# Windowed attention beside a gated feed-forward: the value products of two chunks issued together

## The chip, the cores and the metric

The kernel runs on one NeuronCore of a Trainium2 chip. The metric is the device time of one execution in microseconds (us). Three executions of the kernel before took 825.59, 825.71 and 825.8 us; their median is 825.71 us. TensorE is called PE below, its weight loads PEld, VectorE DVE, ScalarE ACT, GpSimd POOL, and the engine that issues most of the transfers SP.

## The reference

Two branches read the same `x` (2048 rows, 512 columns) and are mixed row by row by a gate.

```python
qkv = (x @ wqkv).reshape(B, S, 3, H, Dh)            # H = 32 heads, Dh = 16
scores = einsum("bhqd,bhkd->bhqk", q, k) * Dh ** -0.5
mask = (i - j >= 0) & (i - j < 256)                 # each row sees itself and the 255 before
a = einsum("bhqk,bhkd->bhqd", softmax(scores), v) @ wo
b = (silu(x @ w_gate) * (x @ w_up)) @ w_down        # 1792 hidden columns
out = g * a + (1 - g) * b                           # g = sigmoid((x * gate_w).sum(-1))
```

Only the attention is touched by the change: the step that multiplies exponentials by values, and what turns its result into the attention's rows.

## The kernel before

Everything is float32; products of full precision are made of three products of split halves. The attention works on 8 groups of four heads (`G`), each over 16 blocks of 128 rows (`NB`). The rows are also counted in chunks of 512 (`NCH` = 4 for each group).

The middle of the kernel is one loop over `t` = 0 to 128 (line 601); `g, i = divmod(t, 16)` gives group and block, and each `t` has four head steps `hd` = 0 to 3. The order on every engine is the order in which the program writes the instructions (line 40). A head step writes, in this order:

- `stage1` of the next group (line 251): one matmul of raw scores (L263) into a `ps1` bank, and on DVE one instruction that adds the mask and takes the row maximum (L265);
- `stage2` of this group (line 293): one matmul of shifted scores, keys on the partitions (L304), into a `ps2` bank, and on ACT the exponential into a tile `pt` (L306). Each block needs two `pt` tiles, one for each pair of heads. After every second head POOL zeroes what lies outside the window (L308, L311);
- three pairs of matmuls of a side job (`lanes`, L215): either the projection of a later group or a piece of the feed-forward's hidden products, in accumulators `pa` and `pb`. A job lasts four `t`: its parts 0 and 2 fill the two `pa` tiles, its parts 1 and 3 the two `pb` tiles;
- whatever has been put in `AT` for this `(t, hd)` by `later`, and one step of `FIN`.

PSUM is shared out by lines 164 to 166: two tiles each under the names `pa`, `pb`, `ps1` and `ps2`, each 128x512 float32.

When a job's last part is over, `copies` (line 515) has ACT move its two tiles to SBUF (L519). For the two `pb` tiles this falls into the first `t` of the next job: the first tile at head step 0, the second at head step 2.

```python
for m in range(2):
    later(t0, 2 * m, lambda m=m: nc.scalar.copy(places[m], ps[m]))
```

At every fourth `t` (part 0, head step 1) `av` (line 316) writes one chunk's value products, "a run": 64 (chunk 0) or 96 small matmuls (L328) on a half of the rows and a quarter of the columns each. The lower half of the keys adds up in a tile `first`, named `pb` (`pa` for the very last run), the upper half in a tile `second`, named `ps2`. A chunk reads the exponentials of the six blocks that end with its own last one, and value tiles `vg` that `load_v` (line 288) fetches from DRAM.

`finish` (line 333) then has five steps: ACT copies `second` to SBUF (L339); DVE adds `first` (L341, and for chunk 0, where the upper half has no first 64 columns, a copy of these, L343); DVE transposes (L346); DVE divides by the sum that stands in column 16 of each head (L350, L351); DVE transposes back (L355) and POOL issues the transfer to `od`. It is a generator; line 616 takes a step of it at `(part, hd)` = (0, 2), (1, 1), (2, 1), (3, 1), after a first one right behind `av`.

The feed-forward's second product and the output projection follow after the loop (from line 638).

Of the kernel before, what the change touches and what calls it, by code (L numbers as in the profile page):

```python
# [9 lines left out]
F32 = mybir.dt.float32  # L10
F32R = mybir.dt.float32r
AF = mybir.ActivationFunctionType
ALU = mybir.AluOpType
# [3 lines left out]
P = 128  # L17
S, D, H, DH, W, F = 2048, 512, 32, 16, 256, 1792
NK = D // P
NB = S // P  # L20
CH = 512
NCH = S // CH
G = H // 4
NF = F // P
VW = 4 * (DH + 1) + DH
# [8 lines left out]
def gated_mix(ctx, tc, xT, xn, w01, wqk, wv, wo, wgu, wd, gw, out):  # L34
# [4 lines left out]
    nc = tc.nc  # L39
# [8 lines left out]
    od = dram.tile([G, P, S], F32, name="od")  # L48
# [40 lines left out]
    def run(gen, n=None):  # L89

        while n is None or n > 0:
            if next(gen, run) is run:
                break
            n = n and n - 1
# [74 lines left out]
    with ExitStack() as A:  # L169
        sm = A.enter_context(tc.tile_pool(name="sm", bufs=2))  # L170
# [59 lines left out]
        def proj(g, c, pool, name, todo=None, los=nc.gpsimd):  # L230

            hf, cc = divmod(c, 2)
            if cc == 0:
                X[g, hf] = x_pair() if g == hf else x_pair(vpool, f"x{g}{hf}")

            def done(ps):
                raw = kept()
                nc.scalar.copy(raw, ps)
                split_qk(g, hf, cc, raw, los)
            return whole(pool, name, todo or products(("p", g), c), done)  # L240

        def stack(g, hf):
            for pr in range(2):
                q, k = (halves_of(t[g % 2][pr])[hf] for t in (QT, KT))
                hi, lo = (x[32 * pr:] for x in X[g, hf])
                for b, (qx, kx) in enumerate(((hi, hi), (hi, lo), (lo, hi))):
                    nc.sync.dma_start(q[b::4].bitcast(F32), qx[:32].bitcast(F32))
                    nc.sync.dma_start(k[b::4].bitcast(F32), kx[64:96].bitcast(F32))

        MX = {}  # L250
        def stage1(g, qb):

            hf, b = divmod(qb, NB // 2)
            if b == 0:
                MX[g, hf] = sm.tile([P, 4, NB // 2], F32, name="mx")
            q0, k0 = qb * P, max(0, qb - 2) * P
            n = q0 + P - k0
            for hd in range(4):
                pr, j = divmod(hd, 2)
                r = slice(64 * j, 64 * j + 63)  # L260

                ps = ps2.tile([P, CH], F32, name="ps2") if g == 0 and pr else ps1.tile([P, CH], F32, name="ps1")
                nc.tensor.matmul(ps[:, :n], QT[g % 2][pr][r, q0:q0 + P], KT[g % 2][pr][r, k0:k0 + n],  # L263
                                 start=True, stop=True)
                mx = nc.vector.tensor_tensor_reduce(out=ps[:, :n], in0=ps[:, :n], in1=mask[:, 3 * P - n:],  # L265
                                                    scale=1.0, scalar=NEG, op0=ALU.add, op1=ALU.max,
                                                    accum_out=MX[g, hf][:, hd, b:b + 1])
                if g == 0:
                    BEHIND.append(mx)
                yield  # L270

        def put_max(g, hf):
            mt = sm.tile([P, 32], F32, name="mt")
            nc.vector.transpose(mt, MX[g, hf].rearrange("p h b -> p (h b)"))
            u = 2 * g + hf
            nc.sync.dma_start(mxd[u], mt)
# [7 lines left out]
                                      v[2 * pr + j:2 * pr + j + 1])  # L284

        VG, PT, AV = {}, {}, {}

        def load_v(n):

            VG[n] = sm.tile([P, 4, VW], F32, name="vg", bufs=4)  # L290
            nc.sync.dma_start(VG[n], vd[n // 4, :, n % 4 * 4:n % 4 * 4 + 4])

        def stage2(g, kb):
# [22 lines left out]
        def av(g, c):  # L316


            AV[g, c] = (pp.tile([P, CH], F32, name="pb" if 4 * g + c + 1 < len(UNITS) else "pa"),
                        ps2.tile([P, CH], F32, name="ps2"))  # L320

            orders = [[4 * c + m for m in ms if 4 * c + m >= 0] for ms in ((0, 1, 2, -1, -2, 3), (0, 1, -1, 2, 3, -2))]
            for n, kbs in enumerate(zip(*orders)):
                for j in range(4):
                    for h, (o, kb) in enumerate(zip(HALVES, kbs)):
                        k0 = kb * P + 64 * h
                        q0, q1 = max(k0, c * CH), min(k0 + W + 64, c * CH + CH)
                        nc.tensor.matmul(AV[g, c][h][32 * j:32 * j + 32, q0 - c * CH:q1 - c * CH],  # L328
                                         VG[4 * g + kb // 4][o, kb % 4, 17 * j:17 * j + 32],
                                         PT[g, kb, j // 2][o, j % 2, q0 - kb * P:q1 - kb * P],  # L330
                                         start=n == 0, stop=n == len(orders[0]) - 1, skip_group_check=True)

        def finish(g, c):


            first, second = AV[g, c]
            both = osb.tile([P, CH], F32, name="on")
            lo = 0 if c else 64
            nc.scalar.copy(both[:, lo:], second[:, lo:])  # L339
            yield  # L340
            nc.vector.tensor_tensor(out=both[:, lo:], in0=first[:, lo:], in1=both[:, lo:], op=ALU.add)  # L341
            if lo:
                nc.vector.tensor_copy(both[:, :lo], first[:, :lo])  # L343
            yield
            ot = osb.tile([P, CH], F32, name="on")
            nc.vector.transpose(ot, both)  # L346
            yield
            v = ot.rearrange("p (s e) -> p s e", e=32)
            rc = osb.tile([P, CH // 32], F32, name="rc", bufs=1)
            nc.vector.reciprocal(rc, v[:, :, DH])  # L350
            nc.vector.tensor_tensor(out=v[:, :, :DH], in0=v[:, :, :DH],  # L351
                                    in1=rc[:, :, None].to_broadcast([P, CH // 32, DH]), op=ALU.mult)
            yield
            on = osb.tile([P, CH], F32, name="on")
            nc.vector.transpose(on, ot)  # L355
            nc.gpsimd.dma_start(od[g, :, c * CH:(c + 1) * CH], on)
            yield

        vp = ExitStack()
        vpool = vp.enter_context(tc.tile_pool(name="vpool", bufs=1))  # L360
# [76 lines left out]
        both = [proj(g, 0, pp, "pa", [(w01raw[:, k, g], xraw[0][k]) for k in range(NK)]) for g in range(2)]  # L437
# [40 lines left out]
        first = chain(*(stage1(0, b) for b in range(NB)))  # L478
# [15 lines left out]
        for c in range(2, NCH):  # L494
            run(proj(1, c, pp, "pb"))
        stack(1, 1)
        for n in range(4):
            load_v(n)
        vp.close()
        ptp = A.enter_context(tc.tile_pool(name="ptp", bufs=13))  # L500
        osb = A.enter_context(tc.tile_pool(name="osb", bufs=2))


        AT = {}
# [1 line left out]
        def later(t, hd, *fs):  # L506
            AT.setdefault((t, hd), []).extend(fs)
# [89 lines left out]

        FIN, tops = iter(()), [(0, 1)]  # L600
        for t in range(G * NB + 1):
            g, i = divmod(t, NB)
            d, part = divmod(t, NSLOT)
            if part == 0:
                turns = unit(UNITS[d], t) if d < len(UNITS) else [iter(())] * NSLOT
            s1 = stage1(g + 1, i) if t < g7 else iter(())
            s2 = stage2(g, i) if t < G * NB else iter(())
            for hd in range(4):
                run(s1, 1)
                if t < g7:  # L610
                    run(s2, 1)
                elif hd % 2 == 0:
                    run(s2, 2)
                run(turns[part], 3)
                if (part, hd) in ((0, 2), (1, 1), (2, 1), (3, 1)):
                    run(FIN, 1)
                for f in AT.pop((t, hd), ()):
                    f()
                if hd == 1 and part == 0:
                    while tops:  # L620
                        top = tops.pop()
                        put_max(*top)
                        later(t + 1, 1, lambda top=top: get_max(*top))
                    if t:
                        ag, c = divmod(d - 1, NCH)
                        av(ag, c)
                        FIN = finish(ag, c)
                        run(FIN, 1)
            if i in (7, 15) and g + 1 < G:
                tops.append((g + 1, i // 8))  # L630
            if t >= 10 and t % 4 == 2 and t + 6 < G * NB:
                load_v((t + 6) // 4)
        run(FIN)
        for key in sorted(AT):
            for f in AT[key]:
                f()
# [1 line left out]
    with ExitStack() as B:  # L638
# [114 lines left out]
        second = []  # L753
        fresh, waiting, ready = [], [(0, n, *first_halves[n]) for n in range(2)], []
        for c, n in seq:
            f = ORDER[n]
            todo, ready, second = ready, second, []
# [58 lines left out]
```

## Time and profile before

| | |
|---|---|
| median of three executions | 825.71 us |
| the profiled execution | 825.82 us |
| its span, first to last instruction | 824.1 us |
| PE busy | 815.9 us (99%) |
| DVE busy | 509.8 us (62%) |
| ACT busy | 451.6 us (55%) |
| POOL busy | 343.1 us (42%) |
| value products (L328), matmuls | 2816 |
| runs of value products | 32, from 95.4 us to 599.6 us |

The span is what the profile sees; 1.7 us of the execution lie around it. Busy PE time is the time in which at least one matmul is under way by the profile; matmuls overlap, so the mean duration of one (346 ns for L328) is longer than the distance from one to the next. In the views of instructions in order of time, the columns are the start, the duration, engine, line, operation, tile written and read, shapes and count, and in brackets the idle time before it with what ended it.

### The profile page before, as it was taken

How to read it: one execution, taken by the hardware profiler on the slowest of the kernel's cores; microseconds unless marked ns; L12 is line 12 of the kernel's file. 1: busy time of each engine (PE TensorE's matmuls, PEld its weight loads, DVE VectorE, ACT ScalarE, POOL GpSimd, SP SyncE). 2: the span in 40 equal slices, each digit the busy share in tenths (PEclk: the TensorE clock that was granted, in tenths of full speed). 3: DMA queues.
4: the chain of work that ended last, by engine and by line, in shares of the span. 5: the costliest groups of instructions: out<-in, count | busy, mean ns of one | idle time of the engine just before them, and what ended most of it. 6: DMA issues, size and time to landing. Idle time of an engine off the chain costs nothing.

```text
span 824.1 us, 21565 instructions
## 1 busy us (share of the span) xinstructions
PE 815.9 (99%) x8306; PEld 677.6 (82%) x8306; DVE 509.8 (62%) x1422; ACT 451.6 (55%) x940; POOL 343.1 (42%) x631
## 2 busy tenths in 40 slices
PE   9999999999999999999999999999999999999998
PEld 6788988888888988887888888877778888888886
DVE  5496677677667676676677677745548443443443
ACT  6422666666666666666666666666647423334341
POOL 5812555555546555555554654456600111011020
PEclk9999999999999999999999999999999999999999
DMA  8484525625634643642652553556769444573621
GB/s 293 111 259 148 167 101 156 180 96 139 195 109 115 188 135 98 183 143 90 181 167 88 172 157 114 147 190 226 248 224 371 158 156 123 165 218 102 213 94 51
DMA packets 70582, 133.27 MB, mean 162 GB/s; under 512 B 14288, under 2 KB 19024, under 8 KB 70480
## 3 DMA queue, kind: packets, MB, share of 16 engines
q1 hardware_dynamic: 66512, 118.00, 46.4%
q0 software_dynamic: 3968, 13.90, 4.6%
q8 instruction: 65, 1.06, 0.5%
q14 instruction: 37, 0.30, 0.1%
HBM read 61.08 MB, written 45.61 MB: 129 GB/s over the span
## 4 chain that ended last, share of the span: by engine, by line
PE 88%; DMA 4%; POOL 3%; DVE 2%; SPq 1%; ACT 1%; issue 1%; ACTq 0%; POOLq 0%
PE pb L215 22%; PE pa L215 22%; PE pb L328 7%; PE ps L263 6%; PE ps L85 6%; PE ps L84 6%; PE ps L83 6%; PE ps L304 4%; PE pb L84 2%; PE pb L85 2%; PE pb L83 2%; PE ps L328 2%; DMA ev<-wd 1%; PE pb L708 1%; PE pa L708 1%
## 5 line engine op out<-in xcount | busy, mean ns | idle before, releaser
L265 DVE CUSTOM_DVE_ANT_0 ps<-ps,mask 128x384 f32<-128x384 f32 (+2 forms) x512 | 272.2, 540 | 142.5 <-PE ps L263 76.8
L306 ACT ACTIVATE pt<-ps 128x384 f32<-128x384 f32 (+2 forms) x512 | 240.8, 477 | 114.9 <-PE ps L263 56.8
L308 POOL TENSOR_SCALAR_AFFINE_SELECT pt<-pt 128x256 f32<-128x256 f32 x256 | 108.2, 423 | 212.5 <-ACT pt L306 204.0
L304 PE MATMUL ps<-q,k 64*128 64x384 f32 (+2 forms) x512 | 162.5, 328 | 0.0
L263 PE MATMUL ps<-k,q 63*128 63x384 f32 (+2 forms) x512 | 158.6, 330 | 0.0
L215 PE MATMUL pb<-xhi,wh 64*128 64x512 f32 x512 | 115.2, 394 | 0.0
L215 PE MATMUL pb<-xlo,wh 64*128 64x512 f32 x512 | 114.0, 391 | 0.0
L215 PE MATMUL pb<-xhi,wl 64*128 64x512 f32 x512 | 113.8, 392 | 0.0
L215 PE MATMUL pa<-xhi,wh 64*128 64x512 f32 x512 | 112.3, 393 | 0.0
L215 PE MATMUL pa<-xlo,wh 64*128 64x512 f32 x512 | 110.9, 391 | 0.0
L215 PE MATMUL pa<-xhi,wl 64*128 64x512 f32 x512 | 110.7, 391 | 0.0
L263 PEld LDWEIGHTS ps<-k,q 63*128 63x128 f32 x512 | 88.8, 185 | 16.1 <-issue 5.4
L311 POOL TENSOR_SCALAR_AFFINE_SELECT pt<-pt 128x256 f32<-128x256 f32 x224 | 98.7, 441 | 0.0
L304 PEld LDWEIGHTS ps<-q,k 64*128 64x128 f32 x512 | 93.0, 185 | 5.6 <-issue 0.8
L712 DVE TENSOR_TENSOR sg<-got,sg 128x512 f32<-128x512 f32 x50 | 44.5, 889 | 51.4 <-ACT sg L711 48.1
L328 PE MATMUL ps<-pt,vg 64*32 64x320 f32 (+4 forms) x1408 | 75.2, 346 | 0.0
L328 PE MATMUL pb<-pt,vg 64*32 64x320 f32 (+3 forms) x1360 | 74.0, 350 | 0.8 <-ACT ev L519 0.7
L265 DVE DVE_READ_ACCUMULATOR2_ANT mx<- 128x1 f32 x512 | 72.1, 141 | 0.0
L328 PEld LDWEIGHTS pb<-pt,vg 64*32 64x32 f32 x1360 | 46.5, 106 | 29.1 <-ACT pt L306 9.9
L215 PEld LDWEIGHTS pb<-xhi,wh 64*128 64x128 f32 x512 | 59.3, 185 | 8.6 <-ACT ev L519 0.3
L215 PEld LDWEIGHTS pb<-xhi,wl 64*128 64x128 f32 x512 | 59.3, 184 | 7.5
L215 PEld LDWEIGHTS pa<-xhi,wl 64*128 64x128 f32 x512 | 56.7, 184 | 7.9
(162 smaller groups left out, 1557.8 us busy)
## 6 DMA issues: line engine op xcount, KB each, us to landing
raws<-ev SPq DMA_DIRECT2D x104, 256.0 KB
got<-raws SPq DMA_DIRECT2D x100, 256.0 KB
od<-on POOLq DMA_DIRECT2D x32, 256.0 KB, 3.1
raw<-wgu SPq DMA_DIRECT2D x28, 256.0 KB
q<-xhi SPq DMA_DIRECT2D x56, 128.0 KB
k<-xhi SPq DMA_DIRECT2D x56, 128.0 KB
vd<-vs POOLq DMA_DIRECT2D x8, 672.0 KB, 5.9
vg<-vd SPq DMA_DIRECT2D x32, 168.0 KB
```

What stands on the lines that cost most here:

```text
L83: nc.tensor.matmul(ps, lh, rh, start=start and i == 0, stop=False)
L84: nc.tensor.matmul(ps, lh, rl, start=False, stop=False)
L85: nc.tensor.matmul(ps, ll, rh, start=False, stop=stop and i == n - 1)
L215: mm = nc.tensor.matmul(ps[me], w[r], x[r], start=not second and i == 0, stop=bool(second) and i == n - 1)
L263: nc.tensor.matmul(ps[:, :n], QT[g % 2][pr][r, q0:q0 + P], KT[g % 2][pr][r, k0:k0 + n], start=True, stop=True)
L265: mx = nc.vector.tensor_tensor_reduce(out=ps[:, :n], in0=ps[:, :n], in1=mask[:, 3 * P - n:], scale=1.0, scalar=NEG, op0=ALU.add, op1=ALU.m ...
L304: nc.tensor.matmul(ps[:, :n], KT[g % 2][pr][r, k0:k0 + P], QT[g % 2][pr][r, k0:k0 + n], start=True, stop=True)
L306: BEHIND.append(nc.scalar.activation(pt[:, j, :n], ps[:, :n], AF.Exp, scale=SCALE))
L308: nc.gpsimd.affine_select(out=pt[:, :, :P], in_=pt[:, :, :P], pattern=[[0, 2], [1, P]], compare_op=ALU.is_ge, fill=0.0, base=0, channel_mu ...
L311: nc.gpsimd.affine_select(out=pt[:, :, 2 * P:], in_=pt[:, :, 2 * P:], pattern=[[0, 2], [-1, P]], compare_op=ALU.is_ge, fill=0.0, base=-1, ...
L328: nc.tensor.matmul(AV[g, c][h][32 * j:32 * j + 32, q0 - c * CH:q1 - c * CH], VG[4 * g + kb // 4][o, kb % 4, 17 * j:17 * j + 32], PT[g, kb, ...
L712: nc.vector.tensor_tensor(out=sg, in0=gu[1], in1=sg, op=ALU.mult)
```

## The change

Chunks 0 and 1 of a group are multiplied at one place: when the eighth block of the group is through (`i` = 8). Chunk 2 stays at `i` = 12 and chunk 3 at `i` = 0 of the next group, so that a group has three runs in place of four. The places of the five steps of `finish` are written out as pairs (distance in `t`, head step); of chunk 0, the copy and the sum stand right behind the two runs, in the order copy of chunk 0, copy of chunk 1, sum of chunk 0. The exponentials of eight blocks and a half must now be kept: 17 tiles `pt` in place of 13. There are 3 buffers `vg` in place of 4, with loads at other times, 3 buffers `on` in place of 2, one fixed tile for the reciprocals, and the scratch for transfers that POOL issues is set to 4096.

```diff
-            VG[n] = sm.tile([P, 4, VW], F32, name="vg", bufs=4)
+            VG[n] = sm.tile([P, 4, VW], F32, name="vg", bufs=3)
...
+            place = {}
+            def copy():
+                both = place[0] = osb.tile([P, CH], F32, name="on")
+                nc.scalar.copy(both[:, lo:], second[:, lo:])
+            def add():
+                both = place[0]
+                nc.vector.tensor_tensor(out=both[:, lo:], in0=first[:, lo:], in1=both[:, lo:], op=ALU.add)
+                if lo:
+                    nc.vector.tensor_copy(both[:, :lo], first[:, :lo])
+            def across():
+                place[1] = osb.tile([P, CH], F32, name="on")
+                nc.vector.transpose(place[1], place[0])
...
+            return copy, add, across, divide, back
...
-        for n in range(4):
+        for n in range(3):
             load_v(n)
         vp.close()
-        ptp = A.enter_context(tc.tile_pool(name="ptp", bufs=13))
-        osb = A.enter_context(tc.tile_pool(name="osb", bufs=2))
+        ptp = A.enter_context(tc.tile_pool(name="ptp", bufs=17))
+        osb = A.enter_context(tc.tile_pool(name="osb", bufs=3))
...
-        FIN, tops = iter(()), [(0, 1)]
+        FIN, tops = {}, [(0, 1)]
+        LOADS = {9: 3, 13: 4, 17: 5, 18: 6}
+
+        def values(t):
+
+            ag, m = divmod(t - 8, NB)
+            if m == 0:
+                cs, times = (0, 1), [((0, 1),) * 2 + ((0, 3), (2, 0), (2, 3)), ((0, 1), (0, 2), (1, 1), (3, 2), (4, 1))]
+            else:
+                cs, times = (1 + m // 4,), [((0, 1), (0, 2), (1, 1), (2, 1), (3, 1))]
+            for c in cs:
+                av(ag, c)
+            for k, steps in enumerate(zip(*(finish(ag, c) for c in cs))):
+                for todo, ts in zip(steps, times):
+                    dt, hd = ts[k]
+                    if (dt, hd) == (0, 1):
+                        todo()
+                    else:
+                        FIN.setdefault((t + dt, hd), []).append(todo)
...
-                if (part, hd) in ((0, 2), (1, 1), (2, 1), (3, 1)):
-                    run(FIN, 1)
+                for f in FIN.pop((t, hd), ()):
+                    f()
                 for f in AT.pop((t, hd), ()):
                     f()
...
-                    if t:
-                        ag, c = divmod(d - 1, NCH)
-                        av(ag, c)
-                        FIN = finish(ag, c)
-                        run(FIN, 1)
+                    if t > 4 and i != 4:
+                        values(t)
...
-            if t >= 10 and t % 4 == 2 and t + 6 < G * NB:
-                load_v((t + 6) // 4)
-        run(FIN)
+            m = (t - 3) % NB + 3
+            if t > 8 and m in LOADS and (t - m) // 4 + LOADS[m] < 4 * G:
+                load_v((t - m) // 4 + LOADS[m])
...
-    nc = bacc.Bacc("TRN2", target_bir_lowering=False, num_devices=1)
+    nc = bacc.Bacc("TRN2", target_bir_lowering=False, num_devices=1, dynamic_dma_scratch_size=4096)
```

`av`, `copies` and the names and numbers of the PSUM tiles are the same before and after.

More of the change, by code (lines that the diff above doesn't have):

```diff
@@ L286, in gated_mix @@
         VG, PT, AV = {}, {}, {}
+        RC = sm.tile([P, CH // 32], F32, name="rc", bufs=1)
         def load_v(n):
-            VG[n] = sm.tile([P, 4, VW], F32, name="vg", bufs=4)
+            VG[n] = sm.tile([P, 4, VW], F32, name="vg", bufs=3)
             nc.sync.dma_start(VG[n], vd[n // 4, :, n % 4 * 4:n % 4 * 4 + 4])
@@ L336, in finish, with divide, back @@
             first, second = AV[g, c]
-            both = osb.tile([P, CH], F32, name="on")
             lo = 0 if c else 64
[L339 to L357, printed above, removed]
+            place = {}
[10 more added lines that the diff above has]
+                nc.vector.transpose(place[1], place[0])
+            def divide():
+                v = place[1].rearrange("p (s e) -> p s e", e=32)
+                nc.vector.reciprocal(RC, v[:, :, DH])
+                nc.vector.tensor_tensor(out=v[:, :, :DH], in0=v[:, :, :DH],
+                                        in1=RC[:, :, None].to_broadcast([P, CH // 32, DH]), op=ALU.mult)
+            def back():
+                on = osb.tile([P, CH], F32, name="on")
+                nc.vector.transpose(on, place[1])
+                nc.gpsimd.dma_start(od[g, :, c * CH:(c + 1) * CH], on)
+            return copy, add, across, divide, back
         vp = ExitStack()
@@ L623, in gated_mix @@
                         later(t + 1, 1, lambda top=top: get_max(*top))
-                    if t:
-                        ag, c = divmod(d - 1, NCH)
-                        av(ag, c)
-                        FIN = finish(ag, c)
-                        run(FIN, 1)
+                    if t > 4 and i != 4:
+                        values(t)
             if i in (7, 15) and g + 1 < G:
                 tops.append((g + 1, i // 8))
-            if t >= 10 and t % 4 == 2 and t + 6 < G * NB:
-                load_v((t + 6) // 4)
-        run(FIN)
+            m = (t - 3) % NB + 3
+            if t > 8 and m in LOADS and (t - m) // 4 + LOADS[m] < 4 * G:
+                load_v((t - m) // 4 + LOADS[m])
+        for key in sorted(FIN):
+            for f in FIN[key]:
+                f()
         for key in sorted(AT):
```

## The prediction

> **What bounds the kernel now.** I read the page's head and its chain first, then the busy time of a stretch out of the loop's middle, then what PE waited for.
>
> ```profile
> span 824.1 us, 21565 instructions
> PE 815.9 (99%) x8306; PEld 677.6 (82%) x8306; DVE 509.8 (62%) x1422; ACT 451.6 (55%) x940; POOL 343.1 (42%) x631
> PE 88%; DMA 4%; POOL 3%; DVE 2%; SPq 1%; ACT 1%; issue 1%; ACTq 0%; POOLq 0%
> ```
> ```profile
> 200.00:300.00 100.00, 100.00 (x1306) 85.81 (x1304) 70.18 (x234) 64.10 (x141) 54.52 (x111) 1.00 0.51 153
> ```
> ```profile
> PE pb L328 <- ACT ev L519: 0.7, 2, 0.4
> ```
>
> In the loop PE is busy 100 of 100 us at full clock (columns: stretch, length, then PE, PEld, DVE, ACT, POOL), DVE 70, ACT 64 and POOL 55. Over the whole kernel the value products let PE wait twice, 0.7 us in all. So in the loop every microsecond that PE gains or loses is one of the kernel's; work added to another engine costs nothing unless it makes PE wait.
>
> **What one run costs beside its products.** The instructions of PE in order of time, first an ordinary step, then the way into and out of a run of chunk 0:
>
> ```profile
> 174.87 0.39 PE L215 MATMUL pb<-xhi,wl 64*128 64x512 f32 x2
> 175.10 0.33 PE L304 MATMUL ps<-q,k 64*128 64x384 f32 x1
> ```
> ```profile
> 160.59 0.41 PE L215 MATMUL pa<-xhi,wl 64*128 64x512 f32 x2
> 160.93 0.45 PE L328 MATMUL pb<-pt,vg 64*32 64x320 f32 x1
> ...
> 162.47 0.42 PE L328 MATMUL pb<-pt,vg 64*32 64x128 f32 x8
> 162.81 0.44 PE L263 MATMUL ps<-k,q 63*128 63x384 f32 x1
> ```
>
> From the last pair of L215 to the next pair of scores it is 0.23 us (174.87 to 175.10); from there to the first value product 0.34 us (160.59 to 160.93). Entering a run costs 0.11 us more than an ordinary step. On leaving, L263 starts at 162.81, 0.08 us before the modelled end of the run's last product (162.47 + 0.42 = 162.89). If the second run followed the first with no wait, one entry and one leaving would be saved. No row shows two runs joined; I bound the leaving by nothing and by as much again as the entry: a gain of 0.11 to 0.22 us for each group, 0.9 to 1.8 us for eight. The products themselves stay: 2816 matmuls before and after.
>
> The Trainium skill has a rule for this saving: "TensorEngine Tiling (Array Packing)", Key Properties, says that changing the tiling mode drains TensorE. The trace agrees in kind, with the 0.11 us above; by that rule alone the change would be a gain of the size just named.
>
> **The second run has no bank to start in.** Each run needs a `pb` tile for its lower half, and there are two (line 164). Look at ACT around this same run:
>
> ```profile
> 159.88 0.58 ACT L519 COPY ev<-pb 128x512 f32<-128x512 f32 x1
> ...
> 163.00 0.53 ACT L339 COPY on<-ps 128x448 f32<-128x448 f32 x1 [2.13 <-PE ps L328]
> ...
> 163.81 0.59 ACT L519 COPY ev<-pb 128x512 f32<-128x512 f32 x1
> ```
>
> The side job's first `pb` tile is copied out ahead of the run, at 159.88 (head step 0), its second behind it, at 163.81 (head step 2), although ACT had stood idle for 2.13 us: ACT keeps the order of the program. At head step 1 one `pb` tile is therefore still full. Neither line 519 nor `later`'s places are in the diff, and `i` = 8 is a part 0 like the others. So chunk 0 takes the free tile, and chunk 1 cannot take the other: its copy stands in ACT's queue behind the copies of both chunks, the second of which waits for chunk 1's own products. What it can have is chunk 0's tile, once DVE has added it up. That the change puts the copy and the sum of chunk 0 ahead of everything else fits. PE then waits, with both runs already in its queue, for copy, sum and (chunk 0 only) the copy of 64 columns. Behind the waiting product stand chunk 1's other 95, and all later matmuls; ACT's copy of chunk 1, its exponentials and DVE's next mask step wait for those in turn.
>
> **The price of that wait.** The chain appears once with DVE idle, at chunk 0 of the last group:
>
> ```profile
> 553.92 0.28 PE L328 MATMUL pb<-pt,vg 64*32 64x128 f32 x2
> ```
> ```profile
> 554.28 0.53 ACT L339 COPY on<-ps 128x448 f32<-128x448 f32 x1 [2.17 <-PE ps L328]
> ```
> ```profile
> 554.85 0.63 DVE L341 TENSOR_TENSOR on<-pb,on 128x448 f32<-128x448 f32 x1 [0.56 <-ACT on L339]
> 555.39 0.21 DVE L343 COPY on<-pb 128x64 f32<-128x64 f32 x1
> ```
>
> How soon PE starts once a copy has released its tile is seen where a run waited for L519:
>
> ```profile
> 583.10 0.59 ACT L519 COPY ev<-pb 128x512 f32<-128x512 f32 x1 [0.27 <-DVE q L68]
> ```
> ```profile
> 583.73 0.10 PEld L328 LDWEIGHTS pb<-pt,vg 64*32 64x32 f32 x1 [0.72 <-ACT ev L519]
> ```
>
> Laid onto the run at 160.93: the copy starts at 163.00 as now and ends at 163.53; the sum starts 0.04 us later (554.81 to 554.85), at 163.57; from its start to the end of L343 it is 0.75 us (554.85 to 555.60), so the tile is free at 164.32; PE starts 0.04 us later (583.69 to 583.73), at 164.36. Today the next step starts at 162.81. PE thus loses 164.36 - 162.81 = 1.55 us, and saves one entry of 0.11 us, since chunk 1's run no longer begins behind L215: 1.44 us net for each group. All eight groups have this place (`t` = 8, 24, ... 120, each with a side job before it), so 8 x 1.44 = 11.5 us. The last group has no stage 1 in its loop; PE is still nearly full there, and 1.44 us is kept for it too.
>
> Nothing hides the wait: PE has no other work ahead of it in order, and no slack after it, since PE was not waiting for anyone. The Trainium skill warns of it in "Perfetto Trace Analysis", Optimizing Tensor Performance: independent matmul groups should rotate through different PSUM banks so that one's evacuation overlaps the next group's matmuls. The change gives that rotation up; today L339's copy runs beside the next step (163.00, behind 162.81).
>
> Bounds for one group: ACT starting at 0.08 us behind the modelled end (554.20 to 554.28) and not 0.11 us (162.89 to 163.00) gives 1.41 us. If the emptied PE pays the entry again, it is 1.55 us. The transposed maxima that DVE takes at the same place stand ahead of the sum and are done during the run; they add nothing. Eight groups: 11.3 to 12.4 us.
>
> **The other steps.** DVE gets its steps closer together: sum of chunk 1 at (8, 2), transpose of chunk 0 at (8, 3), of chunk 1 at (9, 1). What one such step does to the mask steps, which free the `ps1` banks:
>
> ```profile
> 175.10 0.34 PE L263 MATMUL ps<-k,q 63*128 63x384 f32 x1
> ```
> ```profile
> 175.48 0.57 DVE L265 CUSTOM_DVE_ANT_0 ps<-ps,mask 128x384 f32<-128x384 f32 x1 [0.25 <-PE ps L263]
> 175.96 0.14 DVE L265 DVE_READ_ACCUMULATOR2_ANT mx<- 128x1 f32 x1
> ...
> 182.51 0.57 DVE L265 CUSTOM_DVE_ANT_0 ps<-ps,mask 128x384 f32<-128x384 f32 x1 [0.25 <-PE ps L263]
> ...
> 183.00 0.71 DVE L346 STREAM_TRANSPOSE on<-on 128x512 f32<-128x512 f32 x1
> 183.63 0.53 DVE L265 CUSTOM_DVE_ANT_0 ps<-ps,mask 128x384 f32<-128x384 f32 x1
> ...
> 185.12 0.57 DVE L265 CUSTOM_DVE_ANT_0 ps<-ps,mask 128x384 f32<-128x384 f32 x1 [0.24 <-PE ps L304]
> ```
> ```profile
> L263 PEld LDWEIGHTS ps<-k,q 63*128 63x128 f32 x512 | 88.8, 185 | 16.1 <-issue 5.4
> ```
>
> A head step takes 0.87 us (182.51 to 185.12 is three). L265 behind the transpose starts at 183.63 in place of 183.38, 0.25 us late, and a step without extra work makes that up. Sum and transpose in successive steps leave it some 0.5 us late, the next step catches up most, the transpose of chunk 1 adds 0.25 us again. A mask step on time ends 0.57 us after its start, and the same bank is wanted two steps (1.74 us) after the scores that it reads, which start 0.38 us ahead of it (175.10 to 175.48): 1.74 - 0.38 - 0.57 = 0.79 us of room, less 0.19 us for loading the weights, 0.60 us. The lag stays under that; I price it at 0, and at 0.1 us for each of the seven groups with stage 1 at most as part of the likeliest case. The interval at `i` = 4 loses its steps; that is worth 0, DVE having been no limit.
>
> The exponentials: at (8, 2) a `pt` tile of block 0 is wanted again, and chunk 0's run, the only reader, is over; 17 tiles do. `vg`: value tile 3 of a group is loaded at `t` = 9 for `t` = 16, 4 at 13 for 24: cover of over 20 us. The loads wait for the run at `t` = 8 to be over, and what stands behind them on SP's queue is due later still. `on`: six tiles for two chunks in three buffers, each given back a step before it is wanted. The scratch of POOL's transfers touches these:
>
> ```profile
> od<-on POOLq DMA_DIRECT2D x32, 256.0 KB, 3.1
> vd<-vs POOLq DMA_DIRECT2D x8, 672.0 KB, 5.9
> ```
>
> If it held only one transfer of `vd`, POOL would wait once for 5.9 us between the two that are sent together (lines 473 and 474); the rest come farther apart. POOL is 42% busy, so 0; 0 to 1 us in the range.
>
> **Sum.** 825.82 + 11.5 = 837.3 us for a profiled execution. The median of the three executions is 0.11 us lower, so 837.2 us. Own range of this case: 11.3 to 12.4 us for the wait, up to 0.7 us for DVE's lag and 1 us for the scratch, and 1 us below for steps of the chain that run faster with less beside them: 836.0 to 839.8 us.
>
> **Rivals.**
>
> No wait, because the bank is free after all (the change does what its words say). It is one fact: whether the side job's second `pb` tile has been copied out before chunk 1's first product. The job's products are over before head step 0 and ACT idles for 2.13 us during the run, so the copy could be had. Against it stand the rows of L519 at 159.88 and 163.81 and a diff that leaves line 519 alone. From the point at which the tile is free ahead of the run the wait is zero and the two runs save 0.9 to 1.8 us: 823.9 to 824.8 us, 824.3 in the middle, which is within 0.2% (1.65 us, about what a measurement of this kernel can tell from no change). Chance 7%, 2 of them for over 0.2%.
>
> DVE as a second limit. With `ps1` banks freed late, PE waits at L263 at five places in a group (one behind each step of `finish` that follows another). If a mask step behind extra work takes its whole 0.57 + 0.14 us (175.48 and 175.96) and so catches up only 0.16 us a step, the lags pass 0.60 us by 0.1 to 0.2 us each: 0.5 to 0.7 us a group, 3.5 to 5 us for seven, on top of the wait: 840.7 to 842.2 us. For it: the denser places. Against: the mask step at 185.12 waits for PE again after two steps. Chance 6%.
>
> **How the numbers follow.** The likeliest case has 86%, the free bank 7%, DVE's limit 6%, the rest 1%. The range is the likeliest case's, widened to 835.6 below for an over-priced chain and to 841.0 above for the lower end of DVE's case; the free bank is left out. Faster 2%, same 5%, slower 93%.
>
> **What would show it.** In the profile after: value products start at 24 places and not 32; at eight of them a hole of about 1.45 us on PE in the midst of L328 (between the 64th and the 65th product), named as a wait for DVE L343 or L341, 11 to 12 us in all; PE busy falls from 99% to about 97.5% of the span, its busy time nearly unchanged. L339's copies of chunk 0 and the sum behind them lie inside that hole. The forecast is wrong if L519's second copy is found ahead of chunk 1's run, if the hole is missing, or if L263 waits for DVE L265.

## The result, and the profile after

The kernel after takes 838.63 us (median of 4 executions, 837.67 to 840.12) against 825.75 us for the kernel before in the same comparison: a ratio of 1.0156, 95% interval 1.0139 to 1.0173, 11.5 to 14.3 us slower. The profiled execution took 837.67 us. The forecast was 837.2 us in a range of 835.6 to 841.0.

The page of the kernel after; the rows are the span, the engines' busy time and the chain that ended last:

```profile
span 835.9 us, 21558 instructions
PE 814.7 (97%) x8306; PEld 684.0 (82%) x8306; DVE 511.5 (61%) x1422; ACT 452.5 (54%) x940; POOL 341.4 (41%) x631
PE 94%; DMA 2%; issue 2%; DVE 1%; ACT 1%; SPq 0%; ACTq 0%; DVEq 0%
```

The span has grown by 11.8 us while PE's busy time is 1.2 us less than before: PE does the same work and stands still for longer. The waits of PE say where (time in all, times, longest; the value products are L329 here; `issue` means that the profile names nothing that PE waited for):

```profile
PE pb L329 <- issue: 12.5, 8, 1.6
```

Eight waits, one for each group, all on the value products that write `pb`. The same place in the middle of a joined run, second group, on PE, ACT and DVE in order of time:

```profile
177.57 0.42 PE L329 MATMUL pb<-pt,vg 64*32 64x128 f32 x8
179.55 0.43 PE L329 MATMUL pb<-pt,vg 64*32 64x320 f32 x1 [1.56 <-issue]
```
```profile
174.98 0.58 ACT L526 COPY ev<-pb 128x512 f32<-128x512 f32 x1
...
178.13 0.53 ACT L342 COPY on<-ps 128x448 f32<-128x448 f32 x1 [2.16 <-PE pb L329]
182.13 0.59 ACT L342 COPY on<-ps 128x512 f32<-128x512 f32 x1 [3.47 <-PE ps L329]
...
182.99 0.59 ACT L526 COPY ev<-pb 128x512 f32<-128x512 f32 x1
```
```profile
178.69 0.62 DVE L346 TENSOR_TENSOR on<-pb,on 128x448 f32<-128x448 f32 x1 [2.56 <-ACT on L342]
179.23 0.21 DVE L348 COPY on<-pb 128x64 f32<-128x64 f32 x1
```

Read them as one chain: chunk 0's last products end at 177.99, ACT copies from 178.13 to 178.66, DVE adds from 178.69 and ends L348 at 179.44, and PE starts chunk 1 at 179.55. The side job's second `pb` tile (the later row of L526) is copied at 182.99, behind chunk 1's copy at 182.13. The other seven holes have the same length: from the last product of chunk 0 to the first of chunk 1 it is 1.83 us from start to start in each.

### The profile page after: what moved, and what is told of

Same layout as the page of the kernel before. It is cut to its first block, busy times and chain, and to the rows that moved or that the text cites. A ratio compares the mean times of both kernels' runs of the same rounds, so it can differ in the third digit from the quotient of the medians.

```text
span 835.9 us, 21558 instructions
## 1 busy us (share of the span) xinstructions
PE 814.7 (97%) x8306; PEld 684.0 (82%) x8306; DVE 511.5 (61%) x1422; ACT 452.5 (54%) x940; POOL 341.4 (41%) x631
## 4 chain that ended last, share of the span: by engine, by line
PE 94%; DMA 2%; issue 2%; DVE 1%; ACT 1%; SPq 0%; ACTq 0%; DVEq 0%
PE pb L215 23%; PE pa L215 23%; PE pb L329 7%; PE ps L263 6%; PE ps L85 6%; PE ps L84 6%; PE ps L83 6%; PE ps L305 4%; PE pa L195 2%; PE pb L195 2%; PE ps L329 2%; PE pb L84 2%; PE pb L83 2%; PE pb L85 2%; PE pb L733 1%
## 5 line engine op out<-in xcount | busy, mean ns | idle before, releaser
L265 DVE CUSTOM_DVE_ANT_0 ps<-ps,mask 128x384 f32<-128x384 f32 (+2 forms) x512 | 273.2, 540 | 133.3 <-PE ps L263 67.9
L263 PE MATMUL ps<-k,q 63*128 63x384 f32 (+2 forms) x512 | 157.9, 328 | 0.0
L215 PE MATMUL pb<-xhi,wh 64*128 64x512 f32 x512 | 115.7, 394 | 0.4 <-ACT ev L526 0.4
L215 PE MATMUL pb<-xlo,wh 64*128 64x512 f32 x512 | 114.2, 392 | 0.0
L215 PE MATMUL pb<-xhi,wl 64*128 64x512 f32 x512 | 114.0, 392 | 0.0
L215 PE MATMUL pa<-xhi,wh 64*128 64x512 f32 x512 | 113.3, 393 | 0.6 <-ACT ev L526 0.6
L215 PE MATMUL pa<-xlo,wh 64*128 64x512 f32 x512 | 111.9, 391 | 0.0
L215 PE MATMUL pa<-xhi,wl 64*128 64x512 f32 x512 | 111.7, 391 | 0.0
L263 PEld LDWEIGHTS ps<-k,q 63*128 63x128 f32 x512 | 88.8, 185 | 13.9 <-issue 4.0
L329 PE MATMUL pb<-pt,vg 64*32 64x320 f32 (+3 forms) x1360 | 73.8, 350 | 12.7 <-issue 12.5
L329 PEld LDWEIGHTS pb<-pt,vg 64*32 64x32 f32 x1360 | 48.0, 106 | 38.5 <-issue 14.4
L329 PE MATMUL ps<-pt,vg 64*32 64x320 f32 (+4 forms) x1408 | 74.9, 346 | 0.0
L265 DVE DVE_READ_ACCUMULATOR2_ANT mx<- 128x1 f32 x512 | 72.3, 141 | 0.0
L215 PEld LDWEIGHTS pb<-xhi,wh 64*128 64x128 f32 x512 | 59.4, 185 | 8.6 <-ACT ev L526 1.3
L215 PEld LDWEIGHTS pb<-xhi,wl 64*128 64x128 f32 x512 | 59.2, 184 | 6.5
L215 PEld LDWEIGHTS pa<-xhi,wh 64*128 64x128 f32 x512 | 57.7, 185 | 7.8 <-ACT ev L526 1.6
```

The source lines that it names most:

```text
L215: mm = nc.tensor.matmul(ps[me], w[r], x[r], start=not second and i == 0, stop=bool(second) and i == n - 1)
```

## The experiments

The theory: chunk 1 waits for chunk 0's `pb` tile, through one ACT copy and two DVE instructions. The rivals: DVE's closer steps; the changed buffers, loads and scratch; or a cost of running two chunks together that has nothing to do with the bank.

**The bank free in time.** At the eight joined places, the second `pb` tile is copied out one head step earlier, ahead of `av`:

```diff
-                        later(t0, 2 * m, lambda m=m: nc.scalar.copy(places[m], ps[m]))
+                        later(t0, m if hf and t0 % NB == 8 else 2 * m, lambda m=m: nc.scalar.copy(places[m], ps[m]))
```

> The kernel after, but at the eight places of joined runs the side job's second pb tile is copied out at head step 1, ahead of the value products, and not at head step 2. If the bank was the cause, chunk 1 finds a free tile, the hole of 1.83 us in the middle of each joined run goes, and with it 8 x 1.5 us: 823.8 to 825.3 us, a little under the kernel before, since a joined run saves one entry (0.11 us) and perhaps a leaving. If the loss came from the closer steps on DVE, from the smaller scratch or from the other buffers, it stays at 837 to 839 us.

It took 825.07 us against 825.47 us for the kernel before, ratio 0.9994 (0.9983 to 1.0004). The loss is gone with one copy moved. PE and ACT of this kernel, second group:

```profile
176.25 0.42 PE L329 MATMUL pb<-pt,vg 64*32 64x128 f32 x8
176.45 0.45 PE L329 MATMUL ps<-pt,vg 64*32 64x320 f32 x1
```
```profile
173.67 0.58 ACT L526 COPY ev<-pb 128x512 f32<-128x512 f32 x1
174.16 0.49 ACT L307 ACTIVATE pt<-ps 128x384 f32<-128x384 f32 x1
174.55 0.58 ACT L526 COPY ev<-pb 128x512 f32<-128x512 f32 x1
176.78 0.53 ACT L342 COPY on<-ps 128x448 f32<-128x448 f32 x1 [1.66 <-PE ps L329]
```

Both rows of L526 now stand ahead of L342, and the next chunk follows 0.20 us behind the start of the last eight products (1.98 us in the kernel after). DVE's steps, the buffers and the scratch are those of the kernel after, so none of them made the loss. The last group kept a wait, at the entry of its run:

```profile
565.05 0.45 PE L329 MATMUL pb<-pt,vg 64*32 64x320 f32 x1 [0.87 <-ACT ev L526]
```

**All but the joining.** The kernel after with four runs to a group at their old places:

```diff
-            ag, m = divmod(t - 8, NB)
-            if m == 0:
-                cs, times = (0, 1), [((0, 1),) * 2 + ((0, 3), (2, 0), (2, 3)), ((0, 1), (0, 2), (1, 1), (3, 2), (4, 1))]
-            else:
-                cs, times = (1 + m // 4,), [((0, 1), (0, 2), (1, 1), (2, 1), (3, 1))]
+            ag, m = divmod(t - 4, NB)
+            cs, times = (m // 4,), [((0, 1), (0, 2), (1, 1), (2, 1), (3, 1))]
...
-                    if t > 4 and i != 4:
+                    if t:
```

> The kernel after with its 17 tiles of exponentials, 3 value tiles, 3 output buffers, load times and smaller scratch, but with four runs to a group at the places of before, and the steps of the sums as before. If only the joining costs, it takes the time of the kernel before, 825.2 to 826.3 us. If the buffers, the loads or the scratch take part in the loss, it lies between, at 828 us or more.

825.94 us, ratio 1.0005 (0.9995 to 1.0014): the time of the kernel before. 17 tiles, three value buffers, the load times and the smaller scratch cost nothing that shows.

**A shorter chain.** For chunk 0, DVE alone empties the `pb` tile; the upper half is added from PSUM afterwards:

```diff
             def copy():
                 both = place[0] = osb.tile([P, CH], F32, name="on")
-                nc.scalar.copy(both[:, lo:], second[:, lo:])
+                if lo:
+                    nc.vector.tensor_copy(both, first)
+                else:
+                    nc.scalar.copy(both, second)
             def add():
                 both = place[0]
-                nc.vector.tensor_tensor(out=both[:, lo:], in0=first[:, lo:], in1=both[:, lo:], op=ALU.add)
-                if lo:
-                    nc.vector.tensor_copy(both[:, :lo], first[:, :lo])
+                nc.vector.tensor_tensor(out=both[:, lo:], in0=(second if lo else first)[:, lo:], in1=both[:, lo:], op=ALU.add)
```

> The kernel after, but for chunk 0 DVE copies the lower half's tile out by itself and adds the upper half from PSUM afterwards, so that the tile is free after one DVE instruction in place of an ACT copy and two DVE instructions. If PE waits for that tile, the hole shrinks from 1.83 us to 0.95 to 1.15 us, 8 x 0.7 to 0.9 us are gained, and the kernel takes 831.5 to 833.5 us. If the hole comes from something else (a drain, the two runs' own length, DVE's load), nothing changes: 838 us.

833.27 us, ratio 1.0086 (1.0069 to 1.0103), 5.4 us under the kernel after. PE and DVE of this kernel, second group:

```profile
177.29 0.42 PE L329 MATMUL pb<-pt,vg 64*32 64x128 f32 x8
178.56 0.45 PE L329 MATMUL pb<-pt,vg 64*32 64x320 f32 x1 [0.84 <-DVE on L343]
```
```profile
177.81 0.69 DVE L343 COPY on<-pb 128x512 f32<-128x512 f32 x1 [1.95 <-PE pb L329]
178.61 0.62 DVE L349 TENSOR_TENSOR on<-ps,on 128x448 f32<-128x448 f32 x1
```

The distance from the last eight products to the next chunk is 1.27 us, 0.71 us less than in the kernel after; 8 x 0.71 = 5.7 us. PE starts once the one DVE copy is over and before the sum starts (178.61). The span is 4.6 us shorter than in the kernel after (831.3 us), less than that; the last group's joined run is entered 0.35 us later there (0.85 us behind the last L215, 0.50 us in the kernel after). So it is the emptying of this tile that PE waits for, and the kernel's time follows the length of the chain.

**Entries doubled.** The kernel before, with each run but the last cut in two; the second half comes behind the scores of head step 2:

```diff
-        def av(g, c):
+        def av(g, c, half):
...
-            for n, kbs in enumerate(zip(*orders)):
+            cut = len(orders[0]) // 2
+            for n, kbs in list(enumerate(zip(*orders)))[half * cut:half * cut + cut]:
...
+                if hd == 2 and part == 0 and t:
+                    av(ag, c, 1)
+                    run(FIN, 1)
                 run(turns[part], 3)
...
-                        av(ag, c)
+                        av(ag, c, 0)
                         FIN = finish(ag, c)
-                        run(FIN, 1)
```

> The kernel before with each of its 32 runs cut in two, the second half one score pair later: 32 more entries and leavings, the same products. Entry alone was read as 0.11 us; with as much again for leaving it is 0.22 us. So 32 x 0.11 to 0.22 us is added, 829 to 833 us, and some 0.2 us a run more where the ps2 tile comes free later than now, up to 839 us; the distances at the entries are to be read from the trace. If a change of shapes cost nothing, it would stay at 825.7 us.

835.95 us, ratio 1.0122 (1.0104 to 1.0141). It had 31 more entries and leavings (the last run stayed whole), and its span is 834.1 us against 824.1 us: 0.32 us for each cut over the whole kernel. In the middle of the loop, where the last group takes no part, it is 0.37 us for each (table below). On PE, between the halves:

```profile
113.20 0.44 PE L263 MATMUL ps<-k,q 63*128 63x384 f32 x1
113.20 0.44 PE L304 MATMUL ps<-q,k 64*128 64x384 f32 x1
113.57 0.35 PE L330 MATMUL pb<-pt,vg 64*32 64x192 f32 x1
```
```profile
PE pa L175 <- POOL ident masks.py:199: 1.4, 1, 1.4
```

and, for comparison, an ordinary step of the kernel before:

```profile
159.96 0.33 PE L304 MATMUL ps<-q,k 64*128 64x384 f32 x1
...
160.13 0.41 PE L215 MATMUL pa<-xhi,wh 64*128 64x512 f32 x2
```

From the scores it takes 0.37 us to the next product, where an ordinary L215 follows after 0.17 us. The wait row above is the longest that PE has in this kernel, and it lies at its very start (the warming matmuls of L175): no wait for a `ps2` tile took part, which the expectation had allowed for beyond 833 us. The first products behind a run come late too, in the kernel before as well:

```profile
162.81 0.44 PE L263 MATMUL ps<-k,q 63*128 63x384 f32 x1
162.82 0.44 PE L304 MATMUL ps<-q,k 64*128 64x384 f32 x1
163.09 0.40 PE L215 MATMUL pa<-xhi,wh 64*128 64x512 f32 x2
```

From the scores to L215 it is 0.28 us here, 0.11 us more than in the ordinary step. What was added by the cuts is put down to the changing of shapes itself, and the 0.11 to 0.22 us expected of it was too little: the time lay above the 829 to 833 us that went with it.

**The last group's late entry.** In the first experiment's kernel four weight pieces are loaded later in the last group (at its `t` = 9, 10, 11 and 12 in place of 7, 9, 10 and 11), so that none takes a buffer at 7:

```diff
-        for m, t in enumerate((1, 2, 3, 5, 6, 7, 9, 10, 11)):
+        for m, t in enumerate((1, 2, 3, 5, 6, 9, 10, 11, 12)):
```

> The first experiment's kernel (second pb tile copied out ahead of the joined runs), in which the last group still enters its joined run 0.94 us late, because a copy of the side job waits for a buffer ev that holds a weight piece still on its way. Here the piece loaded at the last group's t = 7 is loaded at t = 12 instead. If that piece holds the buffer, the late entry goes and the time is 0.7 to 1.1 us under the first experiment's, 823.9 to 824.4 us. If another piece or the transfers themselves hold it, it stays at 825 us.

824.30 us against 825.85 us, ratio 0.9981 (0.9972 to 0.9990). The late entry went: the run starts 0.32 us behind the last L215, as the others do. With it went a wait of 0.9 us shortly before, at an L215 that writes `pa`. So the load at `t` = 7 held the buffer. The span is 822.8 us against 823.3 us, a gain of 0.5 us only: PE now waits 0.8 us at L215 products that write `pb` (0.3 us in the first experiment), and 2.2 us in place of 1.7 us at L83 and L85, behind the loop.

**Seven groups joined.** The first experiment's kernel, but the last group has its four runs as before:

```diff
-                        later(t0, m if hf and t0 % NB == 8 else 2 * m, lambda m=m: nc.scalar.copy(places[m], ps[m]))
+                        later(t0, m if hf and t0 % NB == 8 and t0 < g7 else 2 * m, lambda m=m: nc.scalar.copy(places[m], ps[m]))
...
-            if m == 0:
+            if t in (g7 + 4, g7 + 8):
+                ag, cs, times = G - 1, ((t - g7) // 4 - 1,), [((0, 1), (0, 2), (1, 1), (2, 1), (3, 1))]
+            elif m == 0:
...
-                    if t > 4 and i != 4:
+                    if t > 4 and (i != 4 or t > g7):
```

> The first experiment's kernel with runs joined in the first seven groups alone; the last group has its four runs at the places of before. If a joined run with a free bank saves one entry and one leaving, 0.25 us as the trace of the first experiment has it (0.20 + 0.32 - 0.23 - 0.045), seven of them give 1.75 us against the kernel before, and the late entry of the last group is gone: 823.4 to 824.2 us. If joining saves nothing, 825.5 us.

823.95 us against 825.85 us, ratio 0.9977 (0.9967 to 0.9988): a little faster than the kernel before, and so than the kernel after. The head of its page:

```profile
span 822.1 us, 21551 instructions
PE 813.6 (99%) x8306; PEld 682.7 (83%) x8306; DVE 510.4 (62%) x1422; ACT 452.2 (55%) x940; POOL 339.6 (41%) x631
```

2.0 us of span are gained. So the joining by itself is a gain, if a small one; the fifth and the sixth experiment's kernels are not told apart by these intervals. The 0.25 us for each join that was expected is too little, as the next table shows: seven joins are worth 2.5 us, of which 0.5 us does not reach the span.

**One stretch in all kernels.** From the first product of chunk 2 in group 0 to that of chunk 2 in group 6 the loop runs six groups, with six joins or, in the fourth experiment, 24 cuts. Neither end is entered late, and in between the profile shows no wait of PE but at the joins. The rows that bound it, in the kernel before and in the kernel after:

```profile
128.22 0.45 PE L328 MATMUL pb<-pt,vg 64*32 64x320 f32 x1
520.25 0.45 PE L328 MATMUL pb<-pt,vg 64*32 64x320 f32 x1
```
```profile
129.40 0.45 PE L329 MATMUL pb<-pt,vg 64*32 64x320 f32 x1
529.90 0.45 PE L329 MATMUL pb<-pt,vg 64*32 64x320 f32 x1
```

| kernel | from | to | us | against before |
|---|---|---|---|---|
| before | 128.22 | 520.25 | 392.03 | |
| after | 129.40 | 529.90 | 400.50 | 1.41 more for each join |
| bank free in time | 128.09 | 517.93 | 389.84 | 0.36 less for each join |
| all but the joining | 127.93 | 519.96 | 392.03 | nothing |
| shorter chain | 129.09 | 525.39 | 396.30 | 0.71 more for each join |
| entries doubled | 128.50 | 529.36 | 400.86 | 0.37 more for each cut |
| seven groups joined | 128.03 | 517.87 | 389.84 | 0.36 less for each join |

A join with a free bank gives back what a cut costs, so the two agree on the price of changing the shapes once there and back. The buffers, loads and scratch change nothing here either.

## Why the prediction was right, point by point

- **PE bounds the loop, so a hole in it is a loss in full.** Right. In the stretch of the table each join costs 1.41 us, which would be 11.3 us for eight; the span grew by 11.8 us. The other 0.5 us lies outside the stretch. In the last group the runs are entered 0.4 us late in all, where it was 1.0 us before, but PE waits there 1.0 us for the side job's copies at L215, which it did not before.
- **The bank.** Right, and shown: with the second tile copied ahead of the run the hole is gone, and with a shorter chain it is shorter.
- **The chain's price.** 1.44 us was forecast and 1.41 us measured, but this closeness is in part luck: two small errors cancel. The loss was forecast at 1.55 us. Measured, it is 1.98 us from the start of the last eight products to the next product, in place of 0.34 us to L263 (162.47 to 162.81 in the kernel before): 1.64 us. Two terms were a little small: ACT starts 0.14 us behind the end of the products (177.99 to 178.13) and not 0.11 us, and PE starts 0.11 us behind the release (179.44 to 179.55) and not 0.04 us. The row of the restart was that of a weight load; here the load comes first (179.52) and the product behind it. Against this the join saves more than the 0.11 us of an entry: the 0.11 us by which the first products behind a run come late are also paid once in place of twice, and the forecast had no term for them. 1.64 - 0.22 us gives 1.42 us.
- **The saving of a joined run.** Mis-sized: 0.11 us was taken, with 0.22 us as its bound. A join with no wait leaves 0.20 us between the start of the last eight products and the next chunk, so it saves 0.34 + 0.11 - 0.20 + 0.11 = 0.36 us, as in the table. In the rival with a free bank the whole of it counts: that rival's 824.3 us would have been 822.8 us and its side "faster". Over the whole kernel this does not show in full: the first experiment's span is only 0.8 us under that of the kernel before, with the late entry in the last group.
- **DVE, buffers, loads, scratch at nothing.** Right: the first two experiments hold them all, and neither shows a cost. No row names a wait of PE for L265 in the kernel after.
- **What would show it.** 24 places, eight holes between the 64th and the 65th product, busy share 97%: as forecast. The label was not: the profile calls the releaser "issue" and not L348, because a separate semaphore instruction in PE's queue takes the wait (in the trace it stands from 177.42 to 179.49); only in the shorter chain does the row name DVE.

The median came out 1.4 us above the forecast. The profiled execution, 837.67 us, is the quickest of four; why the others took up to 2.5 us more is not settled by these runs.

## What to carry to other kernels

Before two blocks of work on the bottleneck engine are put side by side, list the buffers that both hold at once and who empties each of them at that moment: here two blocks needed two `pb` tiles, and one was still waiting for a copy that stood later in ACT's order. A buffer count that suffices for each alone turns into a wait as long as the whole emptying chain. The copy that frees the buffer must stand ahead of the work that needs it, even when its engine looks idle.

## What the runs showed of the hardware

Going from matmuls on 64x128 shapes to 64x32 ones and back costs PE 0.36 us (saved by joining two runs) to 0.37 us (added by cutting a run in two), in the middle of the loop. Only 0.11 us of it is seen at the entry; 0.11 us is seen in the first matmuls behind the run, and the rest in the leaving. The Trainium skill's "TensorEngine Tiling (Array Packing)", Key Properties, says that a change of mode drains TensorE. The rows agree that each change costs time and give it this size; that the cause is a drain no row here shows. And no hole of 1.6 us lowered the granted clock: its mean reads 1.0 over the kernel after, and 0.999 over the kernel before.
